# 1/z folded into the split of the softmax weights, key rows by plain loads, and a new order of the steps

## The chip, the cores and the metric

The kernel runs on one core of a Trainium2 chip. A core has a matrix engine (PE, with its weight loads shown apart as PEld), VectorE (DVE), ScalarE (ACT), GpSimd (POOL), a queue engine (SP) that here only issues DMAs, and sixteen DMA engines that all queues share. Each engine works through its own list of instructions in order; semaphores make it wait for others. SBUF and PSUM have 128 partitions; PSUM has eight banks of 512 fp32 values per partition. The metric is the device time of the whole program in microseconds.

## The reference

Attention over pooled keys is followed by a gated convolution block. The batch is 4, with 12288 queries each and C = 128 channels.

```python
kv_pool = kv.reshape(B, H // 4, 4, W // 4, 4, C).mean(axis=(2, 4))   # 768 keys per batch
k = v = kv_pool.reshape(B, -1, C) @ w_sr
s = (q @ k.transpose(0, 2, 1)) / sqrt(C)
a = exp(s - s.max(-1)); a /= a.sum(-1) + 1e-09
x = a @ v                                                            # attention output
gate = sigmoid(causal 5-tap convolution of x along the sequence, per channel)
out = (gate * (x @ w_val)) @ w_out
```

## The kernel before

The inputs lie channel by channel, so that a tile of queries is 128 channels by 512 queries. 512 queries are a **group**; a batch has 24 groups, the kernel 96. A group has four **tiles** (j = 0 to 3) of 128 queries against all 768 keys.

For one tile PE computes the scores in six matmuls of 384 columns (`score`, L262; q and k are each split into a high and a low part, and three products are added). The scores take two PSUM banks; three such pairs go round. VectorE takes the negated row maximum (`row_max`, L268), ScalarE the exponential in place with its row sum z (`expo`, L280). The weights then go to SBUF as two fp16 parts: the high part by ScalarE (`p_hi`, L327, scaled by 2^15), the low part, what the rounding left, by VectorE (`p_lo`, L331). The low pass is the last reader of the tile's two banks. After every second tile SP issues one DMA transpose of the pair (L335), which writes both parts with keys on the partitions (`pt`). Two groups later PE multiplies them with the values (`av_range`, L344, 18 matmuls of 512 columns into one bank, `av`).

The row sums are not applied to the weights. The four columns z of a group get 1e-9 added by ScalarE (`norm_eps`, L284), are inverted by VectorE (`norm_reciprocal`, L287), turned by PE (`norm_turn`, L290), copied out by VectorE and stored to DRAM (`norm_store`, L297 and L298), and read back by SP as one row of 512 numbers copied to all 128 partitions (`norm_rows`, L303). VectorE multiplies the attention output by it when it forms x (`g_x`, L361).

Then follow, group after group: a copy of four columns from the last group's x by POOL (`new_x`, L357), four taps and four additions by POOL (`g_conv`, L371 and L380), the fifth tap by ScalarE (L369), tanh by ScalarE (L396), the value matmul (`g_val`, L400), the gating by VectorE (`g_h`, L405), the output matmul (`g_out`, L410), its evacuation by ScalarE (`g_evac`, L420) and a store every second group. POOL also forms the low part of a later group's queries (`g_ql`, L248) from the high part that ScalarE casts (`g_qh`, L244).

The order is written out by hand: one pass of the main loop (L481) is one tile, and what each engine gets in this pass stands there in sequence. In pass t the scores of tile t+1 are issued, the row maximum, exponential and high pass of tile t, and the low pass of tile t-1. A group's AV matmuls come two groups behind its scores, its x at the end of that same group, its value and output matmuls four behind.

The keys of the first batch are loaded in 16 pieces and pooled by 16 reductions before the loop (`load_kv`, `pool_kv`). Those of the next batch are made during the current one, one entry of a list (`setup_steps`) per group: two plain loads of 768 KB by SP, six more of 768 KB by POOL's queue that add to the rows already in SBUF, four reductions (`pool_rows`, L138), projection by `w_sr`, and the values with their column scale. `w_moe` arrives as 64-bit numbers and is converted by VectorE in 14 small operations.

Of the kernel before, what the change touches and what calls it, by code (L numbers as in the profile page):

```python
# [15 lines left out]
R = 4  # L16
P = 128
# [10 lines left out]
def attn_moe_kernel(ctx, tc, qT, kvT, w_sr, w_moe, outT):  # L28
# [12 lines left out]
    AV_CUTS = (0, 6, 9, 12, 18)  # L41
    assert 3 * NCH == AV_CUTS[-1]
    PC = NK // PIECES
    QC = NK // 4
# [3 lines left out]
    kvp = ctx.enter_context(tc.tile_pool(name="kvp", bufs=4))  # L48
# [3 lines left out]
    pfp = ctx.enter_context(tc.tile_pool(name="pfp", bufs=3))  # L52
# [14 lines left out]
    zs = [const.tile([P, P], F32, name=f"z{i}") for i in range(3)]  # L67
    for z in zs:
        nc.vector.memset(z, 0.0)
# [4 lines left out]
    def load_moe():  # L74
# [4 lines left out]
        raw = kvp.tile([C, HALF * R], F32, name="rows0", bufs=1).bitcast(I32)[:, :2 * NW]  # L79
        rest = kvp.tile([C, HALF * R], F32, name="rows1", bufs=1)  # L80
# [34 lines left out]
    def load_kv(st, i):  # L115
        t = kvp.tile([C, R, PC * R], F32, name="kvt", bufs=5)
        src = kvT[0].rearrange("r c x -> c r x")
        nc.sync.dma_start(out=t, in_=src[:, :, i * PC * R:(i + 1) * PC * R])
        st["kv", i] = t

    def pool_kv(st, i):
        t = st.pop(("kv", i))
        nc.vector.tensor_reduce(out=st["pool"][:, i * PC:(i + 1) * PC],
                                in_=t.rearrange("c r (k s) -> c k r s", s=R),
                                axis=AX.XY, op=ALU.add)

    def load_rows(b, st, h, r):
        src = kvT[b, r, :, h * HALF * R:(h + 1) * HALF * R]
        if r == 0:
            st["rows", h] = kvp.tile([C, HALF * R], F32, name=f"rows{h}", bufs=1)  # L130
            nc.sync.dma_start(out=st["rows", h], in_=src)
        else:
            nc.gpsimd.dma_start(out=st["rows", h], in_=src, accum_op=ALU.add)

    def pool_rows(st, i):
        t = st["rows", i // 2].rearrange("c (k s) -> c k s", s=R)
        k0 = i % 2 * QC
        nc.vector.tensor_reduce(out=st["pool"][:, i * QC:(i + 1) * QC], in_=t[:, k0:k0 + QC],  # L138
                                axis=AX.X, op=ALU.add)
# [72 lines left out]
    def value_steps(st):  # L212
        return [lambda: trickle.extend(column_scale(st)), lambda: None, lambda: None,
                lambda: values(st, 0, misc()) or split_values(st, 0),
                lambda: values(st, 1, misc()) or split_values(st, 1)]

    def setup_steps(b, st):
        loads = [(h, r) for r in range(1, R) for h in range(2)]
        steps = [lambda: key_tiles(st) or load_rows(b, st, 0, 0) or load_rows(b, st, 1, 0)]
        for h, r in loads:  # L220
            steps += [lambda: None, lambda h=h, r=r: load_rows(b, st, h, r)]
        steps += [lambda i=i: (None, lambda: pool_rows(st, i)) for i in range(4)]
        steps += [lambda h=h: project(st, h, misc()) or split_keys(st, h) for h in range(2)]
        return steps + value_steps(st)

    def load_pair(g, n, parts=1):

        q = io.tile([C, 2, GQ], F32, name="q")
# [42 lines left out]
    def on_pe(j):  # L271

        return j >= NX

    def expo(g, j):
        if j == 0:
            g.z = zs[g.i % len(zs)]
        if on_pe(j):
            g.pf[j] = pfp.tile([P, NK], F32, name="pf")
        nc.scalar.activation(out=halves(g.pf[j]) if on_pe(j) else g.s[j], in_=g.s[j],  # L280
                             func=AF.Exp, bias=g.nm.pop(j), accum_out=g.z[:, j:j + 1])

    def norm_eps(g):
        nc.scalar.activation(out=g.z[:, :NT], in_=g.z[:, :NT], func=AF.Copy, bias=1e-9)  # L284

    def norm_reciprocal(g):
        nc.vector.reciprocal(out=g.z[:, :NT], in_=g.z[:, :NT])  # L287

    def norm_turn(g, m):
        nc.tensor.transpose(m[:, :P], g.z, ident)  # L290
        g.rm = m[:NT, :P]

    def norm_store(g):

        r = small.tile([NT, P], F32, name="r")
        g.rd = dram.tile([NT, P], F32, name="rd")
        nc.vector.tensor_copy(out=r, in_=g.rm)  # L297
        nc.sync.dma_start(out=g.rd, in_=r)  # L298

    def norm_rows(g):  # L300
        g.rb = work.tile([C, GQ], F32, name="rb", bufs=3)
        row = g.rd.rearrange("(o j) p -> o (j p)", o=1)
        nc.sync.dma_start(out=g.rb, in_=row.broadcast_to([C, GQ]))  # L303

    def turn(g, j):

        pf = g.pf.pop(j)
        for k in range(NCH):
            c = k % (NCH // 2) * P
            nc.tensor.transpose(g.s[j][:, k // (NCH // 2), c:c + P], pf[:, k * P:(k + 1) * P],  # L310
                                ident)

    def pt_tile(g):
        if g.pt is None:
            g.pt = ptp.tile([P, NT, 2 * NCH, P], F16, name="pt")
        return g.pt

    def part(g, j, a):

        if on_pe(j):  # L320
            return pt_tile(g)[:, j, a * NCH:(a + 1) * NCH].rearrange("p (h k) q -> p h (k q)", h=2)
        if g.hl is None:
# [307 lines left out]
```

## Time and profile before

| | us |
|---|---|
| median of three runs | 1246.01 (1245.61 to 1255.13) |
| span of the profiled execution | 1239.7 |
| PE busy | 1039.8 (84%) |
| DVE busy | 892.6 (72%) |
| ACT busy | 899.1 (73%) |
| POOL busy | 878.3 (71%) |
| first exponential starts | 31.46 |
| last exponential starts | 1208.25 |

The span is the profiled execution from its first to its last instruction; what a run's time has beyond it lies around the program. A group of rows in the profile reads: line, engine, operation, output and inputs, count | busy time, mean duration in ns of one | idle time of the engine before them and what ended it. A window's row gives the stretch in us, its length, the busy time and count of each engine (or of the instructions asked for), the granted clock of PE, the busy share of the DMA engines (which can exceed 1, since packets overlap) and GB/s.

### The profile page before, as it was taken

How to read it: one execution, taken by the hardware profiler on the slowest of the kernel's cores; microseconds unless marked ns; L12 is line 12 of the kernel's file. 1: busy time of each engine (PE TensorE's matmuls, PEld its weight loads, DVE VectorE, ACT ScalarE, POOL GpSimd, SP SyncE). 2: the span in 40 equal slices, each digit the busy share in tenths (PEclk: the TensorE clock that was granted, in tenths of full speed). 3: DMA queues.
4: the chain of work that ended last, by engine and by line, in shares of the span. 5: the costliest groups of instructions: out<-in, count | busy, mean ns of one | idle time of the engine just before them, and what ended most of it. 6: DMA issues, size and time to landing. Idle time of an engine off the chain costs nothing.

```text
span 1239.7 us, 15458 instructions
## 1 busy us (share of the span) xinstructions
PE 1039.8 (84%) x4598; PEld 674.5 (54%) x4598; DVE 892.6 (72%) x1254; ACT 899.1 (73%) x1659; POOL 878.3 (71%) x966
## 2 busy tenths in 40 slices
PE   2888778699998768779999778769999999899996
PEld 1655445466565445445666545446566666566663
DVE  6966656588886657568888556557888888787784
ACT  1867666588887557668888657656888888788882
POOL 1277667678886668667888667657788888788782
PEclk9989889899999888889999988888999999999998
DMA  7799999999999999999999999999999999999994
GB/s 248 146 217 179 218 192 214 177 213 204 211 219 209 215 174 216 194 182 225 211 225 232 172 192 218 181 169 217 222 211 217 217 213 226 203 230 212 208 221 119
DMA packets 637235, 253.21 MB, mean 204 GB/s; under 512 B 600160, under 2 KB 609120, under 8 KB 637152
## 3 DMA queue, kind: packets, MB, share of 16 engines
q1 hardware_dynamic: 634560, 238.07, 94.8%
q0 software_dynamic: 2592, 14.16, 8.6%
q8 instruction: 37, 0.61, 0.2%
q14 instruction: 46, 0.38, 0.1%
HBM read 75.83 MB, written 25.36 MB: 82 GB/s over the span
## 4 chain that ended last, share of the span: by engine, by line
PE 43%; DMA 28%; DVE 13%; ACT 9%; issue 5%; POOL 1%; SPq 0%; DVEq 0%; ACTq 0%; POOLq 0%
DMA pt<-hl 23%; PE av L344 17%; PE s L262 16%; PE m L400 5%; ACT s L280 4%; DVE nm L268 4%; PE m L410 3%; DVE x L361 3%; DMA rb<-rd 3%; DVE hl L331 3%; ACT hl L327 2%; DMA kvt<-in_kv 1%; DMA q<-in_q 1%; DVE h L405 1%; ACT th L396 1%
## 5 line engine op out<-in xcount | busy, mean ns | idle before, releaser
L344 PE MATMUL av<-pt,vh 128*128 128x512 f16 x1140 | 420.2, 397 | 134.1 <-DMA pt<-hl 102.5
L280 ACT ACTIVATE s<-s,nm 128x768 f32<-128x768 f32 x384 | 335.6, 874 | 257.5 <-DVE z L287 146.4
L331 DVE SCALAR_TENSOR_TENSOR hl<-s,hl 128x768 f16<-128x768 f32 x384 | 363.0, 945 | 25.1 <-ACT hl L327 24.8
L380 POOL TENSOR_TENSOR sum<-sum,tap 128x512 f32<-128x512 f32 x282 | 359.9, 1276 | 26.4 <-ACT tap L369 4.4
L268 DVE TENSOR_REDUCE nm<-s 128x1 f32<-128x768 f32 x384 | 364.3, 949 | 2.6 <-PE s L262 2.6
L371 POOL TENSOR_SCALAR tap<-x,wm 128x512 f32<-128x512 f32 x376 | 253.6, 696 | 149.2 <-DVE x L361 146.9
L327 ACT ACTIVATE hl<-s 128x768 f16<-128x768 f32 x384 | 310.6, 809 | 18.4 <-issue 6.6
L344 PEld LDWEIGHTS <-vh 128*128 128x128 f16 x1164 | 116.5, 100 | 315.2 <-issue 192.2
L262 PE MATMUL s<-kh,qh 128*128 128x384 f32 x768 | 267.0, 430 | 21.2 <-DVE hl L331 15.5
L248 POOL TENSOR_TENSOR ql<-q,qh 128x512 fp32r<-128x512 f32 x96 | 121.6, 1267 | 163.8 <-ACT qh L244 154.1
L344 PE MATMUL av<-pt,vl 128*128 128x512 f16 x570 | 226.2, 397 | 0.0
L262 PE MATMUL s<-kl,qh 128*128 128x384 f32 x768 | 201.6, 344 | 0.0
L361 DVE SCALAR_TENSOR_TENSOR x<-av,down,rb 128x512 f32<-128x512 f32 x95 | 71.3, 751 | 180.1 <-DMA rb<-rd 89.8
L262 PE MATMUL s<-kh,ql 128*128 128x384 f32 x768 | 200.3, 342 | 0.0
L262 PEld LDWEIGHTS s<-kh,qh 128*128 128x128 f32 x768 | 142.9, 199 | 85.3 <-PE m L290 28.0
L262 PEld LDWEIGHTS s<-kl,qh 128*128 128x128 f32 x768 | 144.6, 195 | 0.5 <-DVE kl L163 0.5
L262 PEld LDWEIGHTS s<-kh,ql 128*128 128x128 f32 x768 | 143.3, 193 | 0.0
L380 POOL TENSOR_TENSOR sum<-tap,tap 128x512 f32<-128x512 f32 x94 | 119.8, 1275 | 0.0
L405 DVE SCALAR_TENSOR_TENSOR h<-th,m 128x512 f32<-128x512 f32 x94 | 64.7, 688 | 68.0 <-PE m L400 51.7
L344 PEld LDWEIGHTS <-vl 128*128 128x128 f16 x582 | 58.2, 100 | 88.4 <-issue 67.7
L400 PE MATMUL m<-x,wm 128*128 128x512 f32 x188 | 100.0, 614 | 5.5 <-DVE r L297 5.5
L410 PE MATMUL m<-h,wm 128*128 128x512 f32 x188 | 96.9, 596 | 3.9 <-DVE h L405 3.9
(62 smaller groups left out, 639.9 us busy)
## 6 DMA issues: line engine op xcount, KB each, us to landing
rb<-rd SPq DMA_DIRECT2D x96, 256.0 KB, 3.7
q<-in_q SPq DMA_DIRECT2D x47, 512.0 KB, 5.6
out<-o SPq DMA_DIRECT2D x46, 512.0 KB, 3.8
rows<-in_kv POOLq DMA_DIRECT2D x18, 768.0 KB, 14.5
kvt<-in_kv SPq DMA_DIRECT2D x16, 384.0 KB, 5.7
rows<-in_kv SPq DMA_DIRECT2D x6, 768.0 KB
pt<-hl SPq DMA_TRANSPOSE x192, 6.1
rd<-r SPq DMA_DIRECT2D x96, 2.0 KB
```

What stands on the lines that cost most here:

```text
L248: nc.gpsimd.tensor_tensor(out=g.ql, in0=g.q, in1=g.qh.bitcast(F32), op=ALU.subtract)
L262: nc.tensor.matmul(s[:, h, :HALF], a[:, sl], k[:, h * HALF:(h + 1) * HALF], start=(i == 0), stop=(i == 2))
L268: nc.vector.tensor_reduce(out=nm, in_=g.s[j], axis=AX.XY, op=ALU.max, negate=True)
L280: nc.scalar.activation(out=halves(g.pf[j]) if on_pe(j) else g.s[j], in_=g.s[j], func=AF.Exp, bias=g.nm.pop(j), accum_out=g.z[:, j:j + 1])
L327: nc.scalar.activation(out=part(g, j, 0), in_=g.s[j], func=AF.Copy, scale=2.0 ** 15)
L331: nc.vector.scalar_tensor_tensor(out=part(g, j, 1), in0=g.s.pop(j), scalar=2.0 ** 15, in1=part(g, j, 0), op0=ALU.mult, op1=ALU.subtract)
L344: nc.tensor.matmul(out, g.st[v][:, k * P:(k + 1) * P], g.pt[:, j0:j1, a * NCH + k], start=(i == 0), stop=(i == len(AV_ORDER) - 1))
L361: nc.vector.scalar_tensor_tensor(out=g.x[:, HALO + c0:HALO + c1], in0=av, scalar=g.st["down"], in1=g.rb[:, c0:c1], op0=ALU.mult, op1=ALU.mult)
L371: eng.tensor_scalar(out=g.tap[k], in0=src, scalar1=w, scalar2=1.0, op0=ALU.mult, op1=ALU.mult)
L380: nc.gpsimd.tensor_tensor(out=s, in0=acc, in1=g.tap[k], op=ALU.add)
L400: nc.tensor.matmul(m, wval, g.x[:, HALO + c0:HALO + c1], start=True, stop=True)
L410: nc.tensor.matmul(m, wout, h, start=True, stop=True)
```

## The change

Four things change together.

First, 1/z. Behind each tile's exponential VectorE now forms r = 1/((z + 1e-9) x 2^-15) in two operations on 128 x 1 values (`norm`, an addition with a multiplication, and a reciprocal). The high and low passes take r as their scale per partition where they had the constant 2^15. The addition on ScalarE, the turn on PE, the copy, the store and the broadcast are gone, and `g_x` multiplies by the column scale alone.

Second, the key rows. All batches use `load_kv` and `pool_kv`: eight plain loads of 768 KB on SP's queue, at j = 1 of every second group from the second of a batch on, and 16 reductions, one per group from the fourth on. The accumulating loads on POOL's queue are gone.

Third, the row maximum of tile t+1 is issued in pass t, behind `norm` and the high pass of tile t.

Fourth, the order. A filler on ScalarE (the evacuation, the fifth tap, tanh or the cast of q) stands between the exponential and the high pass of each tile. AV takes 3, 6, 3 and 6 matmuls per pass where it took 6, 3, 3 and 6. x is formed at the start of the next group, the value matmul at j = 2, the gating at j = 3, the output matmul and its evacuation at j = 0. The queries are loaded two groups sooner, into a third buffer, and the conversion of `w_moe` moves behind the first scores.

```diff
-    AV_CUTS = (0, 6, 9, 12, 18)
+    AV_CUTS = (0, 3, 9, 12, 18)
...
-    kvp = ctx.enter_context(tc.tile_pool(name="kvp", bufs=4))
+    kvp = ctx.enter_context(tc.tile_pool(name="kvp", bufs=3))
...
+    def load_kv(b, st, i, n=2):
+        t = kvp.tile([C, R, 2 * PC * R], F32, name="kvt")[:, :, :n * PC * R]
+        src = kvT[b].rearrange("r c x -> c r x")
+        nc.sync.dma_start(out=t, in_=src[:, :, i * PC * R:(i + n) * PC * R])
...
-    def load_rows(b, st, h, r):
-        src = kvT[b, r, :, h * HALF * R:(h + 1) * HALF * R]
-        if r == 0:
-            st["rows", h] = kvp.tile([C, HALF * R], F32, name=f"rows{h}", bufs=1)
-            nc.sync.dma_start(out=st["rows", h], in_=src)
-        else:
-            nc.gpsimd.dma_start(out=st["rows", h], in_=src, accum_op=ALU.add)
...
+    def setup_step(k, b, st):
+        if k == 1:
+            key_tiles(st)
+        if k < PIECES and k % 2 == 1:
+            load_kv(b, st, k - 1)
+        if 3 <= k < 3 + PIECES:
+            pool_kv(st, k - 3)
+        if k == 20:
+            trickle.extend(column_scale(st))
...
-    def norm_eps(g):
-        nc.scalar.activation(out=g.z[:, :NT], in_=g.z[:, :NT], func=AF.Copy, bias=1e-9)
...
-    def norm_turn(g, m):
-        nc.tensor.transpose(m[:, :P], g.z, ident)
...
-        nc.sync.dma_start(out=g.rb, in_=row.broadcast_to([C, GQ]))
...
+    def norm(g, j):
+        g.r[j] = small.tile([P, 1], F32, name="r")
+        z = g.z.pop(j)
+        nc.vector.tensor_scalar(out=z, in0=z, scalar1=1e-9, scalar2=2.0 ** -15,
+                                op0=ALU.add, op1=ALU.mult)
+        nc.vector.reciprocal(out=g.r[j], in_=z)
...
-        nc.scalar.activation(out=part(g, j, 0), in_=g.s[j], func=AF.Copy, scale=2.0 ** 15)
+        nc.scalar.activation(out=part(g, j, 0), in_=g.s[j], func=AF.Copy, scale=g.r[j])
...
-        nc.vector.scalar_tensor_tensor(out=part(g, j, 1), in0=g.s.pop(j), scalar=2.0 ** 15,
+        nc.vector.scalar_tensor_tensor(out=part(g, j, 1), in0=g.s.pop(j), scalar=g.r.pop(j),
                                        in1=part(g, j, 0), op0=ALU.mult, op1=ALU.subtract)
...
-        nc.vector.scalar_tensor_tensor(out=g.x[:, HALO + c0:HALO + c1], in0=av,
-                                       scalar=g.st["down"], in1=g.rb[:, c0:c1],
-                                       op0=ALU.mult, op1=ALU.mult)
+        nc.vector.tensor_scalar_mul(out=g.x[:, HALO + c0:HALO + c1], in0=av,
+                                    scalar1=g.st["down"])
```

The main loop, as the engines see it, is best read from their lists of instructions. First VectorE, a stretch of a group in the middle of the program before, from j = 1 to the next group's j = 0 (nm is the row maximum, hl the low pass, r the copied row of 1/z, h the gating):

```order
L297 COPY r<-m 4x128
L331 SCALAR_TENSOR_TENSOR hl<-s,hl 128x768
L405 SCALAR_TENSOR_TENSOR h<-th,m 128x512
L268 TENSOR_REDUCE nm<-s 128x1
L331 SCALAR_TENSOR_TENSOR hl<-s,hl 128x768
L268 TENSOR_REDUCE nm<-s 128x1
L331 SCALAR_TENSOR_TENSOR hl<-s,hl 128x768
L361 SCALAR_TENSOR_TENSOR x<-av,down,rb 128x512
L268 TENSOR_REDUCE nm<-s 128x1
L287 RECIPROCAL z_103<-z_103 128x4
L331 SCALAR_TENSOR_TENSOR hl<-s,hl 128x768
```

And now, from the end of j = 3 over j = 0 to j = 1 of a group that pools a piece of keys:

```order
L364 SCALAR_TENSOR_TENSOR h<-th,m 128x512
L285 SCALAR_TENSOR_TENSOR hl<-s,r,hl 128x768
L316 TENSOR_SCALAR x<-av,down 128x512
L271 TENSOR_SCALAR z<-z 128x1
L273 RECIPROCAL r<-z 128x1
L259 TENSOR_REDUCE nm<-s 128x1
L285 SCALAR_TENSOR_TENSOR hl<-s,r,hl 128x768
L271 TENSOR_SCALAR z<-z 128x1
L273 RECIPROCAL r<-z 128x1
L259 TENSOR_REDUCE nm<-s 128x1
L120 TENSOR_REDUCE pool<-kvt 128x48
L285 SCALAR_TENSOR_TENSOR hl<-s,r,hl 128x768
```

Each tile now has two small operations between the low pass of the tile before it and the row maximum of the tile behind it; x stands behind the first low pass of a group instead of in front of its first row maximum, and a reduction of keys behind the row maximum of j = 1.

ScalarE, two passes in the middle of the program before (s is the exponential, hl the high pass):

```order
L280 ACTIVATE s,z_102<-s,nm 128x2x384
L327 ACTIVATE hl<-s 128x768
L396 ACTIVATE th<-sum_5138 128x512
L280 ACTIVATE s,z_102<-s,nm 128x2x384
L327 ACTIVATE hl<-s 128x768
L369 ACTIVATE tap_5232<-x,wm 128x512
```

And now:

```order
L264 ACTIVATE s,z<-s,nm 128x2x384
L379 ACTIVATE o<-m 128x512
L281 ACTIVATE hl<-s,r 128x768
L264 ACTIVATE s,z<-s,nm 128x2x384
L323 ACTIVATE tap_10429<-x,wm 128x512
L281 ACTIVATE hl<-s,r 128x768
```

The filler has moved from behind the high pass to in front of it, where the high pass also waits for r.

SP, at the start of a batch's key loads before:

```order
L303 DMA rb<-rd 128x512
L131 DMA rows_3304<-in_kv 128x1536
L131 DMA rows_3306<-in_kv 128x1536
L335 DMA_TRANSPOSE pt<-hl 128x24x128
L298 DMA rd<-r 4x128
L335 DMA_TRANSPOSE pt<-hl 128x24x128
L303 DMA rb<-rd 128x512
L233 DMA q<-in_q 128x1024
```

And now, over two groups:

```order
L290 DMA_TRANSPOSE pt<-hl 128x24x128 x2
L115 DMA kvt<-in_kv 128x4x384
L290 DMA_TRANSPOSE pt<-hl 128x24x128
L224 DMA q<-in_q 128x1024
L290 DMA_TRANSPOSE pt<-hl 128x24x128
L383 DMA out<-o 128x1024
```

The stores of r and the broadcasts have gone from between the transposes, and one key load stands in every second group between two of them.

More of the change, by code (lines that the diff above doesn't have):

```diff
@@ L372, in tap, with add_taps @@
                               op0=ALU.mult, op1=ALU.mult)
+    def add_taps(g, acc, k):
+        s = work.tile([C, GQ], F32, name=f"sum{1 - k % 2}", bufs=1 if k % 2 else 2)
+        nc.gpsimd.tensor_tensor(out=s, in0=acc, in1=g.tap[k], op=ALU.add)
+        return s
     def g_conv(g):
@@ L376, in g_conv, with g_conv_last @@
             tap(g, k, nc.gpsimd)
-        acc = g.tap[0]
-        for i, k in enumerate(range(1, TAPS)):
-            s = work.tile([C, GQ], F32, name=f"sum{i % 2}", bufs=1 + i % 2)
-            nc.gpsimd.tensor_tensor(out=s, in0=acc, in1=g.tap[k], op=ALU.add)
-            acc = s
-        g.gate = acc
+        g.gate = g.tap[0]
+        for k in range(1, TAPS - 1):
+            g.gate = add_taps(g, g.gate, k)
+    def g_conv_last(g):
+        g.gate = add_taps(g, g.gate, TAPS - 1)
     def conv_dve(g, c0=0, c1=GQ):
@@ L479, in drip @@
             trickle.pop(0)()
+    row_max(at(0), 0)
     for t in range(NT * G):
@@ L508, in attn_moe_kernel @@
-        if j == NT - 1:
-            norm_eps(cur)
-            if mg:
-                out_tile(mg)
-                g_evac(mg, mg.m)
-        p_hi(cur, j)
-        if mg and j == 0:
-            mg.th = g_tanh(mg.gate)
+        if og and j == 0:
+            og.m = g_out(og.h, misc())
+        if gi == 1 and j in (0, 1):
+            values(st, j, misc())
+            high, low = split_values(st, j)
+        if ahead is not None and j == 1 and k > 1:
+            high, low = setup_matmul(k, ahead)
@@ L538, in attn_moe_kernel @@
-        if last and j == 3:
-            norm_rows(last)
-        if at(gi + 2) and j == 2:
-            g_qh(at(gi + 2))
+            g_conv_last(xg)
+        if mg and j == 2:
+            mg.th = g_tanh(mg.gate)
+        if j == 3 and at(gi + 2):
+            g_qh(at(gi + 2))
+        norm(cur, j)
+        p_hi(cur, j)
+        if nxt:
+            row_max(nxt, (j + 1) % NT)
+        if high:
+            high()
+            low()
+            high = None
+        if mg and j == 3:
+            mg.h = g_h(mg.th, mg.m)
@@ L542, in attn_moe_kernel @@
+        if ahead is not None and j == 1:
+            setup_step(k, cur.b + 1, ahead)
+        drip()
+        drip()
+        if j == 3 and at(gi + 2):
             g_ql(at(gi + 2))
-        if og and j == 0 and og.i % 2:
+        if og and j == 1 and og.i % 2:
             store_pair(og)
-        if steps and (j == 3 or t < NT):
-            high, low = steps.pop(0)() or (None, None)
     n1, n2, n3, n4, n5 = groups[:-6:-1]
```

205 lines of the change are left out of this document (76 added, 129 removed).

## The prediction

> **What bounds the kernel now.** The page comes first: its span, and which queue holds the DMA engines.
>
> ```profile
> span 1239.7 us, 15458 instructions
> ...
> q1 hardware_dynamic: 634560, 238.07, 94.8%
> ```
>
> Packets of the SP queue fill 94.8% of the sixteen DMA engines, more than any compute engine's share. Next, the stages apart: the same instruction (the high pass, four per group of 512 queries) counted in a stretch of batch 1 while key rows load, and in batch 3, which loads none.
>
> ```profile
> 343.39:545.04 201.65, 48.53 (x60) 0.92 1.09 200
> 993.89:1035.86 41.97, 12.94 (x16) 1.00 1.05 219
> ```
>
> 60 passes are 15 groups: 13.44 us a group while rows load, against 41.97/4 = 10.49 without, and a clock of 0.92 against 1.00. Three batches load so; 2.95 us over 15 groups is 44 us each, 133 us in all. What the DMA engines move shows in a few short windows (last column GB/s).
>
> ```profile
> 369.50:371.50 2.00, 2.00 (x10) 1.38 (x9) 2.00 (x4) 1.81 (x3) 1.92 (x2) 1.00 0.73 136
> 372.00:375.00 3.00, 3.00 (x17) 2.23 (x16) 1.69 (x3) 2.97 (x7) 2.46 (x3) 1.00 1.01 402
> 377.00:379.00 2.00, 0.00 (x0) 0.00 (x0) 1.03 (x2) 0.33 (x2) 2.00 (x3) 1.00 1.27 290
> ```
>
> The first holds the broadcast of 1/z (256 KB), the second plain key rows, the third a transpose of one tile pair (786 KB). So a transpose needs 786/290 = 2.7 us or more, a broadcast 262/136 = 1.9, plain rows 786/402 = 2.0 per load. A group before takes two transposes, a broadcast and half a query load and output store: about 2 x 2.7 + 1.9 + 1.3 = 8.6 at best, and at a share above 1.00 no room is left for accumulating rows. The DMA engines bound the loading stretches; the clean ones are bound by how the compute engines pass work on:
>
> ```profile
> 574.05:585.34 11.29, 10.43 (x49) 6.61 (x47) 9.56 (x14) 9.33 (x17) 9.14 (x11) 1.00 1.07 235
> 993.89:1004.37 10.48, 10.16 (x49) 6.65 (x48) 8.77 (x13) 9.34 (x17) 9.15 (x11) 1.00 1.00 238
> ```
>
> The first group differs from the second by one VectorE reduction (14 for 13) and is 0.81 us longer, though VectorE was idle for 1.7 us of it. That price of a reduction returns below.
>
> **PE and POOL, step by step.** The chain of waits in a clean group gives PE's pieces; POOL's timeline gives its loop.
>
> ```profile
> 996.33 0.86 PE m L400 x2
> 997.19 0.65 PE av L344 x3
> 997.84 1.04 PE s L262 x6
> ```
> ```profile
> 993.29 2.69 POOL L371 TENSOR_SCALAR tap<-x,wm 128x512 f32<-128x512 f32 x4 [1.01 <-DVE x L361]
> 995.95 1.27 POOL L380 TENSOR_TENSOR sum<-tap,tap 128x512 f32<-128x512 f32 x1
> 997.29 3.99 POOL L380 TENSOR_TENSOR sum<-sum,tap 128x512 f32<-128x512 f32 x3
> 1001.49 1.27 POOL L248 TENSOR_TENSOR ql<-q,qh 128x512 fp32r<-128x512 f32 x1 [0.21 <-PE s L262]
> 1002.71 0.19 POOL L357 COPY x<-x 128x4 f32<-128x4 f32 x1
> 1003.77 1.36 POOL L371 TENSOR_SCALAR tap<-x,wm 128x512 f32<-128x512 f32 x2 [0.88 <-DVE x L361]
> ```
>
> After the change PE has four scores, 18 AV matmuls and two 512-wide ones: 4 x 1.04 + 6 x 0.65 + 2 x 0.86 = 9.78 us; the turn of z is gone. POOL's loop is 1003.77 - 993.29 = 10.48, with 0.21 of waiting for qh, so 10.27, and about 10.2 once x no longer multiplies by rb. Neither loop can go below these.
>
> **VectorE and ScalarE, step by step.** These get the added work.
>
> ```profile
> L369 ACT ACTIVATE tap<-x,wm 128x512 f32<-128x512 f32 x94 | 67.2, 714 | 0.0
> L405 DVE SCALAR_TENSOR_TENSOR h<-th,m 128x512 f32<-128x512 f32 x94 | 64.7, 688 | 68.0 <-PE m L400 51.7 <-ACT s L280 13.1 <-ACT hl L327 1.7
> ...
> L396 ACT ACTIVATE th<-sum 128x512 f32<-128x512 f32 x94 | 58.6, 623 | 0.0
> ...
> L287 DVE RECIPROCAL z<-z 128x4 f32<-128x4 f32 x96 | 16.2, 168 | 0.0
> ...
> L181 DVE TENSOR_SCALAR pw<-big 128x1 int32<-128x1 int32 x4 | 0.6, 144 | 0.0
> ```
> ```profile
> 995.80 0.62 ACT L396 ACTIVATE th<-sum 128x512 f32<-128x512 f32 x1
> 996.32 0.87 ACT L280 ACTIVATE s<-s,nm 128x768 f32<-128x768 f32 x1
> 997.11 0.20 ACT L280 ACTIVATION_READ_ACCUMULATOR s<-s,nm 128x1 f32 x1
> 997.34 0.81 ACT L327 ACTIVATE hl<-s 128x768 f16<-128x768 f32 x1
> 998.05 0.72 ACT L369 ACTIVATE tap<-x,wm 128x512 f32<-128x512 f32 x1
> ```
> ```profile
> 998.77 0.95 DVE L331 SCALAR_TENSOR_TENSOR hl<-s,hl 128x768 f16<-128x768 f32 x1
> 999.64 0.95 DVE L268 TENSOR_REDUCE nm<-s 128x1 f32<-128x768 f32 x1
> 1000.82 0.96 DVE L331 SCALAR_TENSOR_TENSOR hl<-s,hl 128x768 f16<-128x768 f32 x1 [0.23 <-ACT hl L327]
> ```
>
> From these starts: exp holds ScalarE for 1.02 us, a 512-wide filler (evacuation, tap, tanh, qh) for 0.5 to 0.6, the high pass for 0.71; a 950 ns VectorE operation holds its engine for 0.87. The high pass now takes its scale from r: the tap, which also reads a scale per partition, takes 714 ns where tanh takes 623, and exp 0.87 where the high pass takes 0.81, so I add 0.07 to each high and low pass. The Trainium skill ("ScalarE: Activation LUTs", What ACT_TABLE_LOAD costs) puts such an operand at about 93 ns: a rule against this change. By it the sum below would be 2 us higher (0.02 in the one step of four that ScalarE closes); the tap's 91 ns bear it out, exp's 0.06 do not quite.
>
> norm is two small operations, 0.14 + 0.17 with a hand-over between: r is there 0.36 us after z, and VectorE is held for 0.28. Now one step from exp's start e, hand-overs put at 0.05: accumulator read at e + 0.99, norm from 1.05, r at 1.41; the filler ends at 1.54, so it covers norm (without it the high pass would start at 1.46 and still be through by 2.3). Row maximum of the next tile 1.33 to 2.28; next exp at 2.34. ScalarE itself is free at 2.33 (2.42 behind the tap). Meanwhile the low pass of the previous tile runs from 0.1 to 1.03, just ahead of norm. Two tiles: 2.34, one: 2.42. Around j=0 VectorE carries h (0.60, at the end of j=3) and x (0.65 by its nearest row, h; 0.58 held): low pass at e + 0.46, x at 1.39, norm at 2.0, row maximum 2.28 to 3.23, next exp at 3.3. A group: 2.34 + 2.34 + 2.42 + 3.3 = **10.40 us**, above POOL's 10.2 and PE's 9.78, whose remaining 0.6 us hides the score's place in the order.
>
> **Key loads.** Eight 768 KB loads per batch stand on SP between transposes, 2.0 us of DMA each, 1.0 a group, in place of the broadcast's 1.9: demand falls to about 2 x 2.7 + 1.3 + 1.0 = 7.7 of 11 us, so the 13.44 should go. Their cost moves to VectorE: 16 reductions per batch instead of 4, in 48 groups. Behind the row maximum at j=1 one delays that tile's low pass to e + 0.64 of the next step, norm to 1.57, the next exp to 2.86: 0.52 each by the working, 0.81 by the measured pair of groups, 0 if idle time takes it. I take 0.52: 25 us.
>
> **The two ends.**
>
> ```profile
> 31.46 0.88 ACT L280 ACTIVATE s<-s,nm 128x768 f32<-128x768 f32 x1 [2.49 <-DVE nm L268]
> ```
> ```profile
> 1208.25 0.87 ACT L280 ACTIVATE s<-s,nm 128x768 f32<-128x768 f32 x1
> ```
>
> The first exp starts at 31.46; the weights' load and conversion move behind it, 261 KB off a stream of 6.3 MB: I take 29 (27 to 32). Behind the last exp lie 31.4 us; the tail loses the 1/z round trip, and gains a group's x and a store: 30 (29 to 34).
>
> **The sum.** 29 + 95.75 x 10.40 (= 996) + 25 + 30 = 1080. Keys' projection, column scale and values add about 4 us a batch, 12 for three. Batch 3 ran from 950.64 on average at (1208.25 - 950.64)/23.75 = 10.85 a group, 0.36 above its clean ones, from transposes that came late; with the DMA relieved I keep a quarter: 9 us. Span 1101. The span before was 1239.7 where the median is 1246.01, so about 6 lie around it: **1107 us**. Its own range: a period of 10.2 takes 19 us off and 10.9 puts 48 on, a reduction at 0 or 0.81 moves it by -25 or +14; not all ends at once, 1075 to 1160.
>
> **Rivals.** (1) VectorE idles as much as before. In the 11.29 group it idled 1.7 us. After, it is held 4 x (0.94 + 0.87 + 0.28) + 0.60 + 0.58 = 9.5; with the same idleness 11.2, and 0.87 more in 48 groups: 29 + 1072 + 42 + 30 + 12 + 6 = 1191. For it: operations in fixed order on two engines that wait for each other in every step; against: fillers now cover the hand-over.
>
> (2) A plain load holds the transpose behind it.
>
> ```profile
> 368.60 0.86 SPq L131 DMA_DIRECT2D rows<-in_kv  x2
> 369.54 8.17 SPq L335 DMA_TRANSPOSE pt<-hl  x1
> ```
> ```profile
> 1002.64 4.05 SPq L335 DMA_TRANSPOSE pt<-hl  x1
> ```
>
> Two loads in a row held the next transpose's issue 4.1 us longer than usual: 2.05 each, 24 loads, 49 us if nothing absorbs it: 1156. The Trainium skill ("DMA: Bandwidth & Descriptors", Queues, rings and completion order) has each ring consumed in order and different queues served in turn; by that the loads, leaving POOL's queue for SP's, stop sharing and go ahead of the transposes. Against: the transpose behind a load is needed a group and a half later.
>
> (3) PE decides, all else hidden: 9.78 a group, 29 + 936 + 30 + 12 + 6 and at most 25 for reductions: 1013 to 1040.
>
> (4) Slower: h, the output matmul and its evacuation now follow one another within j=0 on VectorE, PE and ScalarE, with the high pass queued behind the evacuation. I have the matmul done at e + 1.6, the evacuation gone by 2.2, and 0.3 us to spare. Each microsecond that PE is later there costs every group one. To reach 1258 the average group must be (1258 - 6 - 59 - 12)/95.75 = 12.3, 1.6 above forecast: PE 1.9 us late in each. Against: PE has 0.6 us of slack to catch up.
>
> (5) The loads gain nothing and the loops no more than they cost: 1246, if transposes at 4.05 us of SP per issue, with more between them, set the pace; but two are 8.1 of 10.4.
>
> **Chances.** Forecast 0.60, (1) 0.15, (2) 0.11, (3) 0.05, (4) 0.05, (5) 0.04. One per cent, 12 us, is about what a measurement can tell. All but (4) and (5) are faster: 0.91; same 0.04; slower 0.05. The range takes in the forecast, (1) and (2): 1070 to 1191, leaving out (3) to (5) and the forecast's edges.
>
> **What would show it.** Right: equal group periods near 10.4 in batch 3 and near 10.9 in loading stretches, clock 1.00, SP queue well under 90%, no AV wait on pt; x waiting for POOL's copy or not at all. Wrong: high passes that wait for r (the filler does not cover), VectorE idle above 1.5 us a group (1), transposes issued for 6 us and more behind a kvt load (2), evacuations waiting for the output matmul (4).

## The result, and the profile after

The changed kernel takes 1090.43 us (median of four runs, 1090.10 to 1090.76), the kernel before 1245.81 (median of the three runs shown and a fourth, 1233.85 to 1255.13). The ratio is 0.8803, with a 95% interval of 0.8755 to 0.8851: 12% faster, 17 us below the predicted 1107 and inside the range. How far the reasons held is the subject of the rest. One execution of a later experiment, the changed kernel with accumulating key loads, ran at a granted clock of 0.755 where the other had 0.973, and took 1264.9 us; only the other is used below.

The page of the changed kernel, its span, busy shares and the SP queue's row:

```profile
span 1088.9 us, 15435 instructions
PE 1000.1 (92%) x4502; PEld 643.2 (59%) x4502; DVE 996.2 (91%) x1863; ACT 899.1 (83%) x1564; POOL 864.9 (79%) x947
...
q1 hardware_dynamic: 628608, 226.86, 100.7%
```

The queue's share has *risen*, from 94.8% to 100.7%, where the prediction wanted it well under 90%. Next, the high passes counted by stretch as before (start and end, length, busy time and count, granted clock, DMA share, GB/s): six groups of batch 1 that load and reduce keys, and four of batch 3 that do not.

```profile
434.90:499.63 64.73, 21.59 (x24) 1.00 1.06 220
865.68:906.55 40.87, 14.39 (x16) 1.00 1.05 210
```

64.73/6 = 10.79 us a group and 40.87/4 = 10.22; before it was 13.44 and 10.49. So nearly all of the gain lies in the loading stretches, and the loading groups differ from the clean ones by one reduction, 0.57 us. How long SP was held by issuing a transpose, by tile, fits with this (ns: least, median and most; then the first and last start in us):

```profile
L290 SPq DMA_TRANSPOSE pt<-hl x192: 3522/4436/5931, 38.3 to 1060.9; - x192
```

Of the kernel before the same row, and on its page the row of x:

```profile
L335 SPq DMA_TRANSPOSE pt<-hl x192: 3579/4340/12493, 36.7 to 1213.0; - x192
...
L361 DVE SCALAR_TENSOR_TENSOR x<-av,down,rb 128x512 f32<-128x512 f32 x95 | 71.3, 751 | 180.1 <-DMA rb<-rd 89.8
```

The longest issue of a transpose has gone from 12.5 us to 5.9, and no AV matmul waits for pt any more. The second of these rows stood on the page before the prediction, which did not use it: VectorE's x had waited 89.8 us for the broadcast to land.

The whole of one loading group and one clean group (busy time of PE, PEld, VectorE, ScalarE, POOL, then clock, DMA share, GB/s):

```profile
488.52:499.31 10.79, 10.30 (x48) 6.53 (x47) 10.31 (x20) 9.29 (x18) 9.17 (x11) 1.00 1.09 234
988.21:998.44 10.23, 10.03 (x48) 6.58 (x47) 9.55 (x19) 9.18 (x18) 9.19 (x11) 1.00 0.96 178
```

VectorE idles 0.48 us in the loading group and 0.68 in the clean one. The timelines of the clean group, VectorE and then ScalarE, from the exponential of j = 0:

```profile
988.09 0.68 DVE L364 SCALAR_TENSOR_TENSOR h<-th,m 128x512 f32<-128x512 f32 x1
988.68 1.01 DVE L285 SCALAR_TENSOR_TENSOR hl<-s,r,hl 128x768 f16<-128x768 f32 x1
989.61 0.74 DVE L316 TENSOR_SCALAR x<-av,down 128x512 f32<-128x512 f32 x1
990.27 0.14 DVE L271 TENSOR_SCALAR z<-z 128x1 f32<-128x1 f32 x1
990.44 0.16 DVE L273 RECIPROCAL r<-z 128x1 f32<-128x1 f32 x1
990.52 0.94 DVE L259 TENSOR_REDUCE nm<-s 128x1 f32<-128x768 f32 x1
```

```profile
988.21 0.87 ACT L264 ACTIVATE s<-s,nm 128x768 f32<-128x768 f32 x1
...
990.23 0.60 ACT L379 ACTIVATE o<-m 128x512 f32<-128x512 f32 x1 [1.04 <-PE m L369]
990.72 0.90 ACT L281 ACTIVATE hl<-s,r 128x768 f16<-128x768 f32 x1
991.51 0.88 ACT L264 ACTIVATE s<-s,nm 128x768 f32<-128x768 f32 x1
...
993.02 0.90 ACT L281 ACTIVATE hl<-s,r 128x768 f16<-128x768 f32 x1
993.82 0.87 ACT L264 ACTIVATE s<-s,nm 128x768 f32<-128x768 f32 x1
```

The step of j = 0 takes 991.51 - 988.21 = 3.30 us and the next 993.82 - 991.51 = 2.31. In j = 0 the work on VectorE is unbroken: h, low pass, x, z, r; r is ready at 990.60, and only then can the high pass go (990.72), which the next exponential follows; the row maximum of the next tile is done at 991.46, 0.05 us before that exponential starts. In the other steps ScalarE is unbroken: exponential, filler, high pass, next exponential.

### The profile page after: what moved, and what is told of

It reads as the page before. It is cut to its first block, busy times and chain, and to the rows that moved or that the text cites. A ratio compares the mean times of both kernels' runs of the same rounds, so it can differ in the third digit from the quotient of the medians.

```text
span 1088.9 us, 15435 instructions
## 1 busy us (share of the span) xinstructions
PE 1000.1 (92%) x4502; PEld 643.2 (59%) x4502; DVE 996.2 (91%) x1863; ACT 899.1 (83%) x1564; POOL 864.9 (79%) x947
## 3 DMA queue, kind: packets, MB, share of 16 engines
q1 hardware_dynamic: 628608, 226.86, 100.7%
## 4 chain that ended last, share of the span: by engine, by line
DVE 58%; ACT 29%; PE 5%; issue 5%; DMA 2%; ACTq 0%; SPq 0%; DVEq 0%
DVE hl L285 26%; ACT hl L281 19%; DVE nm L259 11%; ACT s L264 6%; DVE x L316 6%; DVE r L273 4%; DVE pool L120 4%; DVE z L271 2%; PE av L299 2%; ACT tap L323 2%; DVE h L364 2%; PE s L253 2%; ACT th L355 2%; DMA kvt<-in_kv 2%; PE m L359 0%
## 5 line engine op out<-in xcount | busy, mean ns | idle before, releaser
L299 PE MATMUL av<-pt,vh 128*128 128x512 f16 x1140 | 403.6, 381 | 39.0 <-DVE z L271 38.0
L285 DVE SCALAR_TENSOR_TENSOR hl<-s,r,hl 128x768 f16<-128x768 f32 x384 | 389.4, 1014 | 39.6 <-ACT hl L281 39.6
L281 ACT ACTIVATE hl<-s,r 128x768 f16<-128x768 f32 x384 | 345.6, 900 | 60.7 <-DVE r L273 49.2
L259 DVE TENSOR_REDUCE nm<-s 128x1 f32<-128x768 f32 x384 | 360.3, 938 | 1.4 <-PE s L253 1.4
L253 PE MATMUL s<-kh,qh 128*128 128x384 f32 x768 | 282.9, 449 | 9.6 <-DVE z L271 9.2
L299 PE MATMUL av<-pt,vl 128*128 128x512 f16 x570 | 216.1, 379 | 0.0
L379 ACT ACTIVATE o<-m 128x512 f32<-128x512 f32 x94 | 56.1, 597 | 87.1 <-PE m L369 87.1
L369 PE MATMUL m<-h,wm 128*128 128x512 f32 x188 | 102.6, 628 | 9.2 <-DVE h L364 6.8
L359 PE MATMUL m<-x,wm 128*128 128x512 f32 x188 | 96.0, 592 | 0.0
L273 DVE RECIPROCAL r<-z 128x1 f32<-128x1 f32 x384 | 62.9, 164 | 13.1
```

The costliest lines, as they stand in the source:

```text
L253: nc.tensor.matmul(s[:, h, :HALF], a[:, sl], k[:, h * HALF:(h + 1) * HALF], start=(i == 0), stop=(i == 2))
L259: nc.vector.tensor_reduce(out=nm, in_=g.s[j], axis=AX.XY, op=ALU.max, negate=True)
L273: nc.vector.reciprocal(out=g.r[j], in_=z)
L281: nc.scalar.activation(out=part(g, j, 0), in_=g.s[j], func=AF.Copy, scale=g.r[j])
L285: nc.vector.scalar_tensor_tensor(out=part(g, j, 1), in0=g.s.pop(j), scalar=g.r.pop(j), in1=part(g, j, 0), op0=ALU.mult, op1=ALU.subtract)
L299: nc.tensor.matmul(out, g.st[v][:, k * P:(k + 1) * P], g.pt[:, j0:j1, a * NCH + k], start=(i == 0), stop=(i == len(AV_ORDER) - 1))
```

## The experiments

The question was which of the four parts freed the transposes, and whether the steps run as computed. The runs without 1/z and those with the keys of batch 0 leave work out, so their output is another; they are here for their time. Times are medians with the span of the runs in brackets; the interval belongs to the ratio to the kernel before, which took 1242 to 1247 us (medians) beside them.

| what was run | us | ratio to before |
|---|---|---|
| before, no store and broadcast of 1/z | 1127.8 (1126.8 to 1128.8) | 0.907 (0.895 to 0.920) |
| before, plain key loads on SP | 1184.4 (1183.2 to 1185.6) | 0.953 (0.940 to 0.966) |
| before, keys of batch 0 throughout | 1113.5 (both) | 0.896 (0.884 to 0.908) |
| changed, keys of batch 0 throughout | 1047.2 (1046.2 to 1048.1) | 0.843 (0.831 to 0.854) |
| changed, dummy broadcast on SP | 1163.8 (1163.6 to 1164.0) | 0.937 (0.928 to 0.946) |
| changed, plain 256 KB load instead | 1118.4 (1115.7 to 1121.1) | 0.895 (0.885 to 0.906) |
| changed, dummy broadcast on ScalarE's queue | 1124.0 (1116.6 to 1131.4) | 0.903 (0.894 to 0.912) |
| changed, accumulating key loads | 1129.4 (one execution) | none |
| changed, plain key loads on POOL's queue | 1101.9 (1094.7 to 1109.1) | 0.885 (0.877 to 0.894) |
| changed, fillers behind the high pass | 1199.9 (1199.7 to 1200.1) | 0.966 (0.956 to 0.975) |
| changed, row maximum in its own step | 1126.1 (1125.5 to 1126.8) | 0.906 (0.897 to 0.915) |
| changed, x on ScalarE at j = 0 | 1058.7 (1056.5 to 1060.6) | 0.850 (0.846 to 0.855) |

### One part of the change at a time, on the kernel before

**The broadcast gone.**

```diff
-        g.rd = dram.tile([NT, P], F32, name="rd")
-        nc.sync.dma_start(out=g.rd, in_=r)
...
-        nc.sync.dma_start(out=g.rb, in_=row.broadcast_to([C, GQ]))
+        g.rb = one
```

> The kernel before without the store of the row 1/z and without its broadcast from DRAM; x is multiplied by a constant tile instead, so the output is not normalised; every other operation stays. Theory (accumulating loads at fault): the clean groups lose their late transposes (batch 3 from 10.85 to about 10.5), the loading groups stay above 12.5: about 1200 to 1235. Rival (the DMA engines were full, and the broadcast's 1.9 us per group was the part too much): loading groups fall to about 11 and the whole to about 1110.

1127.8 us: 116 us less than the 1244 beside it, by two DMAs a group, near the rival's 1110 and far from the expected 1200 to 1235. The high passes of batch 1's loading stretch and of twenty groups of batch 3:

```profile
362.55:535.75 173.20, 48.48 (x60) 0.98 1.09 212
877.14:1087.20 210.06, 64.64 (x80) 1.00 1.03 198
```

173.20/15 = 11.55 a group and 210.06/20 = 10.50. In these groups of batch 3 no transpose is late any more (its average was 10.85), and the loading groups keep one of the three microseconds: they are 10.5 long, but 11 to 15 where accumulating loads stand.

**Plain key loads, the broadcast kept.**

```diff
+    def load_two(b, st, i):
+        t = kvp.tile([C, R, 2 * PC * R], F32, name="kv2", bufs=3)
+        src = kvT[b].rearrange("r c x -> c r x")
+        nc.sync.dma_start(out=t, in_=src[:, :, i * PC * R:(i + 2) * PC * R])
...
-        steps = [lambda: key_tiles(st) or load_rows(b, st, 0, 0) or load_rows(b, st, 1, 0)]
...
+        steps = [lambda n=n: step(n) for n in range(PIECES + 2)]
```

> The kernel before with one part of the change alone: key rows of later batches by eight plain 768 KB loads per batch on SP's queue and 16 reductions, in place of two plain and six accumulating loads and 4 reductions; 1/z, its broadcast and the old order stay. Theory (the accumulating loads on POOL's queue were what slowed the transposes): the loading groups fall from 13.44 us to about 10.5 + 0.8 for the reduction = 11.3, so 45 groups x 2.1 = 96 us off 1246: about 1150. Rival 1 (the DMA engines are simply full, whoever loads): plain rows and the broadcast together still jam, 1200 or more. Rival 2 (a plain load holds the transposes behind it): 13 us and more a group, 1246 or more.

1184.4 us, between the expected 1150 and the first rival's 1200, and about half of what the broadcast's removal gave. Its transposes by tile, and the wait:

```profile
L346 SPq DMA_TRANSPOSE pt<-hl x192: 3529/4270/8739, 37.6 to 1157.0; - x192
...
  PE av L355: 85.2, 47
```

The longest issue is shorter than before (8.7 us for 12.5), but waits of AV for pt stay: groups alternate between 11.3 and 12 to 17 us, long where a key load stands. That is rival (2), which does not show in the changed kernel. With the broadcast there as well, transposes are late where a plain load stands.

**No key loads at all**, on both kernels.

```diff
-    states = [dict() for _ in range(B)]
+    states = [dict()] * B
...
-        ahead = states[cur.b + 1] if cur.b + 1 < B else None
+        ahead = None
```

> The kernel before with the keys and values of batch 0 used for all four batches: no key loads, reductions, projections after the start, so the output of batches 1 to 3 is another. What the loading stretches cost in the kernel before, as I worked it out, is 133 us, and 22 more for 4 reductions, projection and values in three batches: about 1090. If the loading stretches were slow for another reason than the loads, it stays above 1200.

> The changed kernel with the keys and values of batch 0 for all four batches, as in the run beside it: all groups at the 10.22 us of its batch 3: 31.8 + 95.75 x 10.22 + 31.4 + 1.5 = 1043. Against the same edit of the kernel before this gives what 1/z and the order are worth where no keys are loaded: 1090 - 1043, some 47 us, if the theory is right that most of the gain came out of the loading stretches; if the order is the main gain, the two differ by more than 100 us.

Before: 1113.5, where about 1090 was expected; changed: 1047.2, for 1043. Without any key load the kernel before still has AV wait for pt, 62.2 us in 51 waits, and its groups scatter from 10.5 to 13, one of 15. The changed kernel without key loads, in batch 1 (forty passes, ten groups), and its queue's row:

```profile
322.38:424.54 102.16, 35.96 (x40) 1.00 1.06 207
```

```profile
q1 hardware_dynamic: 615936, 207.98, 100.5%
```

10.22 us a group, at a share of 100.5% and with no AV wait for pt. A share of packet time at 100% is therefore no sign that transposes must wait. Of the 66 us between these two kernels 96 x (10.50 - 10.22) = 27 are the shorter clean period; the rest, by subtraction, is what the broadcast does by itself.

### The broadcast put back into the changed kernel

Each group gets a store of 4 x 128 numbers and a broadcast of them that nothing reads. The first edit puts both on SP; the second replaces this broadcast by a plain load of the same 256 KB; the third has store and broadcast issued by ScalarE's queue at j = 0.

```diff
+        if gi > 0 and j == 1:
+            rd = dram.tile([NT, P], F32, name="rd")
+            nc.sync.dma_start(out=rd, in_=rr)
+        if gi > 0 and j == 3:
+            rb = work.tile([C, GQ], F32, name="rb", bufs=3)
+            row = rd.rearrange("(o j) p -> o (j p)", o=1)
+            nc.sync.dma_start(out=rb, in_=row.broadcast_to([C, GQ]))
```
```diff
-            nc.sync.dma_start(out=rb, in_=row.broadcast_to([C, GQ]))
+            nc.sync.dma_start(out=rb, in_=qT[xg.b, :, xg.t0:xg.t0 + GQ] if xg else qT[0, :, :GQ])
```
```diff
...
+                nc.scalar.dma_start(out=rb, in_=row.broadcast_to([C, GQ]))
+            rd = dram.tile([NT, P], F32, name="rd")
+            nc.scalar.dma_start(out=rd, in_=rr)
```

> The changed kernel with the two DMAs of 1/z put back: per group a 2 KB store to DRAM and its broadcast to 128 x 512, at the same two steps as before, of constant data that nobody reads. Theory (the broadcast between the transposes is what made them late, in whatever order the engines work): most of what the broadcast cost the kernel before (1244 - 1128 = 116 us) comes back: 1150 or more, with AV waiting for pt. Rival (the new order leaves the transposes time enough; the broadcast cost only where someone read its tile or where the order was tight): within 10 us of 1090.

> The changed kernel with the same dummy store of 4 x 128 numbers per group on SP at j=1, and at j=3, in place of the dummy broadcast, a plain load of 128 rows of 2 KB (the same 256 KB, each partition from its own place in the queries). Nothing reads it, the result is complete. Issue list on SP, bytes and places are those of the kernel with the dummy broadcast, which took 1163.8 us where the changed kernel takes 1090. Theory A (the cost is in how the broadcast moves, 128 copies of one 2 KB row at 136 GB/s, where plain rows ran at 402): most of the 73 us goes, 1095 to 1115 us, and transposes are no longer waited for. Theory B (the cost is that two more issues and 256 KB stand between the transposes, of whatever kind): 1145 to 1165 us, with waits of AV for pt near the 66.6 us, 31 times of the dummy broadcast.

> The changed kernel with the store and broadcast of 1/z put back as dummies, but issued by ScalarE's queue, at j=0 where ScalarE waits about 1 us for the output matmul anyway. On SP's queue the two cost 73 us. Theory A (SP's list was too full: it spent 92% of the span issuing in every kernel with the broadcast and 71 to 85% in those without, and each transpose is issued in order behind the rest): the cost goes, 1090 to 1110. Theory B (the DMA engines or the memory are slowed by the 1/z row's transfer itself, whoever issues it): the cost stays, 1150 or more, with AV waiting for pt.

Over the 1090.4 of the changed kernel: 73 us for the broadcast on SP, 28 for the plain load, 34 for the broadcast on ScalarE's queue. The high passes of batch 3 (92 passes, 23 groups), where no key loads stand, with the broadcast and with the plain load, and the queue's row of each page in the same order:

```profile
870.81:1122.68 251.87, 82.86 (x92) 0.99 1.04 214
```
```profile
836.00:1074.68 238.68, 82.83 (x92) 1.00 1.09 225
```
```profile
q1 hardware_dynamic: 643048, 251.96, 102.7%
```
```profile
q1 hardware_dynamic: 643048, 251.96, 105.5%
```

10.95 and 10.38 us a group, where the changed kernel has 10.23. The plain load moves the same bytes, in the same number of packets, issued at the same place, and at the higher share and rate it costs little in batch 3; most of its 28 us lie in the stretches with key loads, where groups of 11 to 14.8 us come back. So 45 of the 73 us go with the way the broadcast moves, between my two theories. SP's list does not set the two apart: issuing fills 92% of the span with the broadcast and 91% with the plain load. The packets do: in batch 3 the 128 packets of a broadcast are spread over 2.6 us on average, those of a plain load over 1.7 us (22 groups each). That this extra microsecond is what delays the transposes is not shown. With the dummy broadcast AV waits for pt (66.6 us, 31 times), though nothing waits for the broadcast itself; with the plain load it is 31.4 us, 21 times:

```profile
L292 SPq DMA_TRANSPOSE pt<-hl x192: 3613/4436/6610, 38.0 to 1136.4; - x192
...
  PE av L301: 66.6, 31
```

No single issue is long (6.6 us at most): transposes arrive late without a long issue. The broadcast issued on ScalarE's queue costs 39 us less than on SP, and what is left sits in a few groups of 12 to 20 us, nearly all in the loading stretches (AV waits for pt 34.3 us, 11 times, up to 7.0), with most groups at the undisturbed 10.20 to 10.24 and 10.79. Its place in the group moved too, so queue and place are not told apart.

### The key loads put back, or onto another queue

```diff
+            nc.gpsimd.dma_start(out=st["rows", h], in_=src, accum_op=ALU.add)
...
+        if 3 <= k <= 13 and k % 2 == 1:
+            n = (k - 3) // 2
+            load_rows(b, st, n % 2, n // 2 + 1)
+        if 14 <= k < 18:
+            pool_rows(st, k - 14)
```
```diff
-        nc.sync.dma_start(out=t, in_=src[:, :, i * PC * R:(i + n) * PC * R])
+        (nc.gpsimd if b else nc.sync).dma_start(out=t, in_=src[:, :, i * PC * R:(i + n) * PC * R])
```

> The changed kernel with the old key loads: two plain and six accumulating loads on POOL's queue per batch, 4 reductions instead of 16. 36 reductions fewer give back 36 x 0.57 = 20 us. Without the broadcast, the old order still lost about 45 us in its loading groups (groups of 12 to 16 us beside others of 10.5). If the stalls are the accumulating loads' own, whatever the order: 1090 - 20 + 45 = 1115, groups of 12 us and more at the loads. If the new order gives the transposes the slack to absorb them: 1070 to 1080, faster than the changed kernel.

> The changed kernel with the plain key loads of batches 1 to 3 issued by POOL's queue, same tiles and sizes, no accumulation. The accumulating loads made groups of 11 to 26 us and cost about 39 us net, 59 with the reductions they save. If it was the accumulation (each packet read, added and written back), plain loads on that queue cost nothing: 1085 to 1100. If it was the second queue beside the transposes, groups of 12 us and more come back: 1120 or more.

With accumulating loads: 1129.4 us in one execution. That is 39 us more, although 36 reductions fewer, at 0.57 us each, should have saved 21. By tile:

```profile
L308 SPq DMA_TRANSPOSE pt<-hl x192: 3523/4418/18197, 37.2 to 1099.5; - x192
...
  PE av L317: 56.3, 20
```

Issues of up to 18.2 us and groups of up to 26: accumulating loads stall transposes by themselves. Plain loads on POOL's queue mostly do not: 1101.9 us, 1094.7 in one execution and 1109.1 in the profiled one. There nearly every group is like the changed kernel's but for a pair in batch 2, 18.4 and 20.2 us long: 17 us of excess, with one transpose's issue of 12.7 us. Why that pair was hit stays open. Most of the cost goes with the accumulation, then, and not with the second queue, though a second queue was no better than SP's in these runs. The two edits also differ in the shape of the loads, but the packets point the same way: on POOL's queue an accumulating packet of 6 KB took 478 ns (median) and a plain one of 4.6 KB 178, on SP's queue a plain one of 6 KB 234.

### The order

**Fillers behind the high pass**, as before the change.

```diff
+        norm(cur, j)
+        p_hi(cur, j)
...
-        norm(cur, j)
-        p_hi(cur, j)
```

> The changed kernel with ScalarE's fillers (evacuation, tap, tanh, cast) behind the high pass again, in front of which ScalarE then has nothing to do while VectorE forms r. By the step: r is there 1.41 us after the exponential's start, high pass 1.50 to 2.30, filler to 2.83, where the next exponential starts now at 2.30: 0.53 in each of three steps, about 0.5 at j=0: 2.1 a group, 200 us: about 1290, slower than the kernel before. Rival (ScalarE has 17% idle time and takes it up elsewhere; VectorE closes the step): 1090 to 1120.

1199.9 us: 109 more, about midway between the expected 1290 and the rival's 1120. The chain of waits in one pass of batch 3:

```profile
1022.97 0.89 ACT s L264 x2
1023.88 0.17 DVE z L271
...
1024.07 0.17 DVE r L273
...
1024.33 0.90 ACT hl L281
1025.23 0.52 ACT th L355
1025.74 0.89 ACT s L264 x2
```

Between the end of the exponential, its accumulator read included (1023.86), and the high pass (1024.33) ScalarE now waits 0.47 us for norm; the step is 2.77 us. Three steps of four grow by that, j = 0 does not: 11.68 us a group. And in these groups a reduction costs next to nothing, 11.71 with one:

```profile
470.02:540.27 70.25, 21.61 (x24) 1.00 0.98 203
935.30:1098.80 163.50, 50.42 (x56) 1.00 0.92 180
```

70.25/6 and 163.50/14. Here ScalarE closes the steps later, and VectorE has room for the reduction.

**Row maximum in its own step.**

```diff
-    row_max(at(0), 0)
+        row_max(cur, j)
...
-        if nxt:
-            row_max(nxt, (j + 1) % NT)
```

> The changed kernel with the row maximum of a tile at the head of its own step again instead of the end of the step before. VectorE's list differs only where something stood behind the row maximum: the gating h at j=3, a key reduction at j=1 and the small operations of the setup now go ahead of it. By the step the low pass and x, not the exponential, hold norm at j=0, so h ahead costs nothing; a reduction ahead delays the next exponential by up to 0.87 where it cost 0.57: 0 to 15 us: 1090 to 1105. Rival (the row maximum ahead is what makes the short step): 0.6 us a group, 1145 or more.

1126.1 us, 36 more, where 0 to 15 was expected. Clean groups keep 10.22. Loading groups become 11.02 (0.23 more), those with the projection of keys 12.1 to 13.4. The page's row of the exponential, with its idle time, and below it that of the changed kernel:

```profile
L264 ACT ACTIVATE s<-s,nm 128x768 f32<-128x768 f32 x384 | 335.6, 874 | 119.7 <-DVE nm L259 119.1
```
```profile
L264 ACT ACTIVATE s<-s,nm 128x768 f32<-128x768 f32 x384 | 335.1, 873 | 2.5 <-DVE nm L259 2.5
```

The wait for the maximum has grown from 2.5 us to 119. The maximum one step ahead is worth nothing in a clean group, and pays in these groups, where VectorE gets extra work.

### A version that goes further

The critical j = 0 has h, low pass, x and norm in a row on VectorE. x goes to ScalarE there, the evacuation to j = 1, and POOL copies the four columns of the last group's x at the end of the group before. The matmuls for the next batch's keys move behind AV.

```diff
+            nc.scalar.activation(out=g.x[:, HALO + c0:HALO + c1], in_=av, func=AF.Copy,
+                                 scale=g.st["down"])
...
+            expo(cur, j)
+            g_x(xg, xg.av, eng=nc.scalar)
...
-        if og and j == 0:
+        if og and j == 1:
...
+        if j == 3 and avg:
+            new_x(avg, xg, nc.gpsimd.tensor_copy)
```

> The changed kernel with x formed by ScalarE (a copy with a scale per partition) behind the exponential of j=0, the evacuation moved to j=1 ahead of the tap, POOL's copy into x ahead of the low part of q, and the setup's matmuls behind AV. VectorE's step at j=0 loses x: r there at e + 1.74, high pass 1.80 to 2.6, row maximum done 2.59, next exponential at 2.65 in place of 3.29. ScalarE at j=1 takes two fillers: 2.8 in place of 2.3. A group 2.65 + 2.8 + 2.3 + 2.3 = 10.05, and a key reduction at j=1 is nearly hidden (0.15): 31.8 + 962 + 7 + 16 + 31.4 + 1.5 = 1050, 4% below the changed kernel. Rival (POOL's or PE's list closes the group at 10.2): 1060 to 1085.

1058.7 us, for an expected 1050, 2.9% below the changed kernel and 15% below the one before. A stretch with reductions and one without:

```profile
431.40:461.80 30.40, 10.80 (x12) 1.00 1.10 235
827.62:927.81 100.19, 36.00 (x40) 1.00 1.08 210
```

30.40/3 = 10.13 and 100.19/10 = 10.02 us: the reduction now costs 0.11. Both are near what was computed (10.05 and 0.15); what is over lies in the groups that make the keys and values of the next batch, up to 14.0 us. One of the latter groups, by engine:

```profile
847.34:857.36 10.02, 10.02 (x48) 6.52 (x47) 8.89 (x18) 9.74 (x19) 9.14 (x11) 1.00 1.13 185
```

PE is busy throughout, which makes it the likely next bound; that was not tested.

## Why the prediction was right, and where its steps failed

**The period: right, by other steps.** Forecast 10.40 us, measured 10.22; with a reduction 10.92 and 10.79. j = 0 is 3.30 us, as worked out, and its list runs as described, but its last link is norm and the high pass on ScalarE, with the row maximum done 0.05 us sooner; high passes wait for r 49.2 us in all, exponentials for the maximum 2.5. The other three are 2.30 each, for 2.34, 2.34 and 2.42, and the step by which VectorE closes two of them through the row maximum failed: ScalarE closes all three, since a filler can start 0.87 us behind the exponential (992.38 behind 991.51 at j = 1) and not 1.02. The 1.02 had been read off a high pass of the kernel before (997.34 behind 996.32), which is no filler.

```profile
992.38 0.73 ACT L323 ACTIVATE tap<-x,wm 128x512 f32<-128x512 f32 x1
```

The operand that is read per partition costs about what the Trainium skill ("ScalarE: Activation LUTs", What ACT_TABLE_LOAD costs) gives, 93 ns: the high pass went from 809 to 900. I had taken 70. On VectorE the same change made the low pass 945 to 1014, 69 ns, for which I had taken 70. The rows of the page before, then those of the changed kernel's, with the evacuation's:

```profile
L331 DVE SCALAR_TENSOR_TENSOR hl<-s,hl 128x768 f16<-128x768 f32 x384 | 363.0, 945 | 25.1 <-ACT hl L327 24.8
...
L327 ACT ACTIVATE hl<-s 128x768 f16<-128x768 f32 x384 | 310.6, 809 | 18.4 <-issue 6.6
```
```profile
L285 DVE SCALAR_TENSOR_TENSOR hl<-s,r,hl 128x768 f16<-128x768 f32 x384 | 389.4, 1014 | 39.6 <-ACT hl L281 39.6
...
L281 ACT ACTIVATE hl<-s,r 128x768 f16<-128x768 f32 x384 | 345.6, 900 | 60.7 <-DVE r L273 49.2
...
L379 ACT ACTIVATE o<-m 128x512 f32<-128x512 f32 x94 | 56.1, 597 | 87.1 <-PE m L369 87.1
```

**The stalls gone: right; their cause: wrong.** The 13.44 went, as the step on key loads said, but the reason behind it failed in its first step, "the DMA engines bound the loading stretches" at a share where "no room is left". The changed kernel runs at 100.7%, with the dummy plain load at 105.5%, and the least disturbed groups of all stand at shares like 1.06. So "SP queue well under 90%" failed too. The prices of the single transfers were no better founded: the window read as the broadcast at 136 GB/s holds 82 of its 128 packets and 17 packets of key rows beside them. That the stalls went all the same is in part luck, since the change also took out the transfer that mattered most. The weights failed too: I gave the gain mainly to the key loads, and counted the broadcast as 1.9 us of a sum. Alone the broadcast's removal gives 116 us where the whole change gives 155, plain loads alone 60. They overlap, because either stalls a group that the other would have stalled: accumulating loads do it by themselves, and so does the broadcast; plain key loads on SP do it only where another 256 KB a group moves beside them, as a broadcast or, less, as a plain load. The 89.8 us that x waited for the broadcast may be why its removal is worth more before (116) than its return costs after, where nothing reads it (73); this is argued, not shown.

**Terms of the sum.** The period: 95.75 x 0.18 = 17 us too high. Reductions: 48 x 0.05 = 2 too low. The start: 31.8 us for 29, and the tail 31.4 for 30, together 4 too low; moving the conversion of `w_moe` did not bring the first exponential forward. Late transposes: 9 us kept, none came, batch 3 ran at 10.23. Around the span: 6 us, where 1090.68 - 1088.9 leaves 1.8 and every profiled run leaves as much; the 6 had mixed the spread between runs into it. Keys' projection: 12, and its groups show 5.4 to 5.7 a batch, 17. All these together, -17 + 2 + 4 - 9 - 4 + 5 = -19, lead from 1107 to 1088. The 2 us left fit the first three groups, 34.0 us where three clean ones are 30.7: VectorE now has the conversion of `w_moe` there, until 61 us.

**The rivals.** (1) VectorE idles 0.68 us a clean group and 0.48 a loaded one, under the 1.5 that it needed. (2) is absent here and present as soon as the broadcast, or its plain stand-in, is back beside plain key loads. By the Trainium skill ("DMA: Bandwidth & Descriptors", Queues, rings and completion order) loads on SP's ring go ahead of the transposes behind them, and on a ring of their own take turns with them: the runs with plain loads on POOL's queue gained nothing by this, 1101.9 us for 1090.4. (3) did not decide: PE is busy 10.03 of 10.23 us, more than the 9.78 that I added up. (4) Its sign is there, evacuations wait for the output matmul 87.1 us in all, and they start at e + 2.02, e being 988.21, where I had the matmul done at e + 1.6. But the evacuation has let go of ScalarE at 990.72 and r is ready at 990.60, so it costs at most 0.1 us a group and not the 1.9 that would have made the kernel slower. The extra version takes both out of that step. (5) fell.

**The filler as cover: right.** "Without it the high pass would start at 1.46 and still be through by 2.3" was right in its first half: without cover norm costs 0.47 us in three steps of four. The second half forgot that the filler must still run behind the high pass, before the next exponential.

What stays open: by which mechanism the broadcast delays transposes. Its issues are short, the same bytes as a plain load explain 28 of 73 us, and the queue it is issued on matters, or its place in the group. The fold of 1/z alone, in the old order, was not run, so what it costs there is not known; with the fillers behind the high pass, as in the old order, it costs 0.47 us in three steps of four.

## What to carry to other kernels

A busy share of the DMA engines near 100% says nothing about what a transfer delays: take one kind of transfer out, and put it back, before pricing it by bytes. A row that names who waits for a landing (here x for the broadcast) can point at the one to try first, but it does not price it: the dummy broadcast cost 73 us though nobody waited for it. A small operation between two engines is free exactly where another job covers it, so the order decides its price, and after each gain the longest step, here j = 0, is the next place to look.

## What the runs showed of the hardware that was not expected

- 256 KB as 128 copies of one 2 KB row, with a small store, cost 73 us over 95 groups; 256 KB as 128 different rows, with the same store and issued at the same place, 28.
- The busy share of packets reached 105.5% over a whole execution, with 227 GB/s on average, and 1.13 in a single group that ran undisturbed; here it was no measure of saturation.
- Loads that accumulate in SBUF held a transpose's issue for up to 18.2 us; the same rows by plain loads on the same queue left nearly all groups untouched.
- One of the 48 key reductions on VectorE cost its group 0.57 us in the changed kernel, 0.03 with the fillers behind the high pass, and 0.11 with x on ScalarE.
- A scale per partition in place of a constant costs ScalarE 91 ns and VectorE 69 ns on 128 x 768.
